# Four attention layers on one core: the values' weights loaded block by block, the first weights issued ahead, and PSUM banks dealt out anew

## The chip, the cores and the metric

The kernel runs on one core of a Trainium2 chip. The metric is the device time of one execution in microseconds, the median of several runs. The engines are TensorE (PE: matmuls, with PEld for its weight loads), VectorE (DVE), ScalarE (ACT), GpSimd (POOL) and SyncE (SP), whose queue issues every DMA of this kernel.

## The reference, cut to what matters

Four layers in the order A, B, A, B, each added to its input. Both normalise x (2048 tokens by 576 features), project to 32 heads of 18 features, and attend over all tokens; A has keys and values per head, B one key and one value head for all.

```python
def _A_ref(x, wqkv, wo):
    qkv = transpose((x @ wqkv).reshape(B, S, 3, H, Dh), 2, 0, 3, 1, 4)
    q, k, v = qkv[0], qkv[1], qkv[2]
    p = softmax(einsum("bhqd,bhkd->bhqk", q, k) * (Dh ** -0.5))
    o = einsum("bhqk,bhkd->bhqd", p, v)
    return transpose(o, 0, 2, 1, 3).reshape(B, S, D) @ wo

def _B_ref(x, wq, wk, wv, wo):          # k = x @ wk, v = x @ wv: one head
    ...

x = x + _A_ref(_layernorm(x), A_wqkv, A_wo)
x = x + _B_ref(_layernorm(x), B_wq, B_wk, B_wv, B_wo)
x = x + _A_ref(_layernorm(x), A_wqkv, A_wo)
x = x + _B_ref(_layernorm(x), B_wq, B_wk, B_wv, B_wo)
```

## The kernel before, in words

**Tiling.** The tokens lie in 16 chunks of 128 (`xo`), and the projections take them in four groups T of 512. Every operand of a projection is kept as two rounded parts, hi and lo (ten slots of 128 features: 0 to 4 hi, 5 to 9 lo), and a product of the two is 14 matmuls (`TERMS`, L31), the hi products first, those that need lo later. So each weight block that comes in by DMA (`raw`) is split by two instructions: a copy to hi (`copy`, L137 on ACT or L139 on POOL) and a subtraction to lo (L161). `load_w` (L142) does this for one block; with `spare` the split is put into the list `splits` and done when `finish_loads` (L172) is called, and without it right away.

**A chunk's way into a layer.** `stats` (L241) takes a chunk's mean and variance on DVE and the reciprocal root on POOL, `scaled` (L253) writes the normalised chunk on DVE (L256, L257), `trans` (L296) transposes it on PE in five matmuls: four into a bank of the tag e (L208) and the fifth into the bank `oacc` (L209). `split_rows` (L197) then makes hi on ACT (L200, L201) and lo on DVE (L202, L203). `advance` does one `trans` and then calls `ready`, which does statistics and scaling for two chunks ahead, and statistics for one more.

**Projections.** `project(T, t)` (L360) makes 128 rows of queries and keys for 512 tokens: 14 matmuls into a bank of the tag m (or e, for fillers), hi by ACT (L375), lo by DVE (L381; for fillers by ACT and POOL), and the store to memory on SP. In layer A the values come from `natural` (L212), 14 matmuls of 288 columns for half a chunk's features (L216), evicted by ACT (L420 or L423). In layer B the values come out of the projection t=4 and are transposed by `v_trans` (L408) into columns 128 to 255 of `oacc` (L410) and copied by DVE (L411).

**Attention.** In 704 phases per layer PE computes scores twice (L497 for the maxima that DVE takes, L506; L638 for the exponentials that ACT takes, L642) and multiplies by the values into `oacc` (L663). The order is written out by hand (`ORDERS`, `todo`, `weave`).

**Output.** `out_w(c)` (L278) projects a chunk of the attention's output in two halves by `natural`, each into an m tile of its own, and DVE adds each half to `xo` (L282). `out_t` (L268) prepares hi and lo of the next two chunks (L137 on ACT, L274 and L276 on DVE). The generator `outs` runs through the 16 chunks, and behind chunk 8 and chunks 9, 11, 13 and 15 it already does `ready` and `advance` for the next layer.

**Banks and buffers.** PSUM has eight banks: `oacc`, three of tag e, and two pairs of tag m (`mtile2`; `mtile` uses the first bank of a pair). SBUF tiles `ptile` are a ring of 15 (tag p), which holds raw weights, evicted projections (`ev`), exponentials and more.

**The opening.** Layer 0 loads x chunks 0 to 3, makes chunks 0 and 1 ready, and then loads `wqkv`'s three parts for queries and keys (five blocks each) by `load_a`, with copies on ACT and subtractions on POOL; between the parts it runs halves of the first two projections. At T=0 of both A layers all five blocks of the values' weights (`load_wsm`, two halves each) are loaded and split on POOL ahead of the first projection of the loop.

All engines run their instructions in the order of the program (`manual_schedule`).

Of the kernel before, what the change touches and what calls it, by code (L numbers as in the profile page):

```python
# [17 lines left out]
DH = D // H  # L18
# [50 lines left out]
def tile_kernel(ctx: ExitStack, tc: tile.TileContext, A_x, A_wqkv, A_wo, B_x, B_wq, B_wk, B_wv, B_wo, out):  # L69
# [62 lines left out]
    def ptile(name, shape=(P, 512), dt=F32):  # L132
        return pool.tile(list(shape), dt, tag="p", bufs=15, name=name)
# [7 lines left out]

    def load_w(c, dsts, srcs, n, hi, lo, spare):  # L142

        raw = pool.tile([P, 640], F32, tag="xh", bufs=2, name="raw") if spare else ptile("raw")
        if sum(s_.shape[1] for s_, _ in srcs) < n:
            nc.gpsimd.memset(raw[:, :n], 0.0)
        for s_, c0 in srcs:
            k = s_.shape[1]
            if c < 4:
                nc.sync.dma_start(raw[:, c0:c0 + k], s_[c * P:(c + 1) * P, :])  # L150
            else:
                nc.sync.dma_start(raw[:64, c0:c0 + k], s_[4 * P:, :])
                nc.sync.dma_start(raw[64:, c0:c0 + k], s_[4 * P:, :])

        def split():
            r = P if c < 4 else 64
            for dst, c0, k in dsts:
                w = dst.shape[1]
                rw = raw[:, c0:c0 + w * k].rearrange("p (w n) -> p w n", w=w)
                copy(hi, dst[:, :, c, :], rw)  # L160
                lo.tensor_tensor(dst[:r, :, 5 + c, :], rw[:r], dst.bitcast(F32)[:r, :, c, :], op=OP.subtract)  # L161
                if c == 4:
                    nc.gpsimd.memset(dst.bitcast(F32)[64:, :, 9, :], 0.0)

        if spare:
            splits.append(split)
        else:
            split()

    splits = []  # L170

    def finish_loads():  # L172
        while splits:
            splits.pop(0)()

    def load_wsm(c, src, hi=nc.gpsimd, lo=nc.gpsimd, spare=False):
        for h in range(2):
# [31 lines left out]
        nc.tensor.transpose(ps1[:, :P], last, ident)  # L209
        return ps4.rearrange("p (c t) -> p c t", t=P), ps1[:, :P]  # L210

    def natural(lhs, h, tile_f):  # L212

        ps = tile_f("psn")[:, :288]
        for i, (xc, wc) in enumerate(TERMS):
            nc.tensor.matmul(ps, lhs[:, xc, :], wsm[:, wc, h * 288:(h + 1) * 288],  # L216
                             start=i == 0, stop=i == len(TERMS) - 1)
            beat()
        return ps
# [21 lines left out]
    def stats(c):  # L241
        xc = xo[:, c, :]
        st = pool.tile([P, 2, nc.vector.BN_STATS_DIM], F32, name="st")
        for i in range(2):
            nc.vector.bn_stats(st[:, i, :], xc[:, i * 288:(i + 1) * 288])  # L245
        mv = pool.tile([P, 2], F32, bufs=4, name="mv")
        nc.vector.bn_aggr(mv, st)
        rs = pool.tile([P, 2], F32, bufs=4, name="rs")
        nc.gpsimd.tensor_scalar(rs[:, 0:1], mv[:, 1:2], EPS, None, op0=OP.add)
        nc.gpsimd.tensor_tensor(rs[:, 1:2], rs[:, 0:1], mhalf, op=OP.pow)  # L250
        return c, mv, rs
# [25 lines left out]

    def out_w(c):  # L278
        ot = ots_[c // 2][:, :, c % 2 * P:(c % 2 + 1) * P]
        for h in range(2):  # L280
            cs = slice(h * 288, (h + 1) * 288)
            nc.vector.tensor_tensor(xo[:, c, cs], natural(ot, h, mtile), xo[:, c, cs], op=OP.add)  # L282

    ors, ots_, lts, rls = {}, {}, {}, {}
    xhs = {}
# [10 lines left out]
    def trans(c):  # L296
        xh = xhs.pop(c)
        split_rows(xt_of(c), *transposed(xh, xh[:, 512:640]))


    at_chunk = {"stats": 0, "scaled": 0, "trans": 0}

    def ready(ahead=1):

        n = min(at_chunk["trans"] + 2, NCH)
        for what, m in (("stats", n), ("scaled", n), ("stats", min(n + ahead, NCH))):
            while at_chunk[what] < m:
                c = at_chunk[what]
                xhs[c] = stats(c) if what == "stats" else scaled(*xhs.pop(c))
                at_chunk[what] += 1  # L310

    def advance(n=1, ahead=1):
        for _ in range(n):
            trans(at_chunk["trans"])
            at_chunk["trans"] += 1
        ready(ahead)

    tail = []

# [28 lines left out]
    for layer in range(4):  # L348
# [56 lines left out]
        vts, half_done = [], {}  # L405

        def v_trans(T, vt):
            pv = oacc[:, P:2 * P]  # L408
            for u in range(4):
                nc.tensor.transpose(pv[:, u * 32:u * 32 + DH], vt[64:82, u * P:(u + 1) * P], ident[64:82, 64:82])  # L410
            nc.vector.tensor_copy(vs[0][:, 4 * T:4 * T + 4, 0, :DH],  # L411
                                  pv.rearrange("p (u e) -> p u e", u=4)[:, :, :DH])

        def v_dst(c, h):
            return v_of(c)[:, 16 * h:16 * h + 16, :DH]

        def project_v(c, h, tile_f, stage=None):
            pv = natural(xt_of(c), h, tile_f)
            if stage is None:
                nc.scalar.activation(v_dst(c, h), pv.rearrange("p (e d) -> p e d", d=DH), AF.Copy)  # L420
            else:
                stage.append((c, h, ptile("vst", (P, 288))))
                nc.scalar.activation(stage[-1][2], pv, AF.Copy)  # L423

# [95 lines left out]
        nc.gpsimd.memset(vs[0][:, :, :, DH:], 1.0)  # L522
        at_chunk.update(stats=0, scaled=0, trans=0)
        if layer == 0:
            ready(0)
            advance(2, 0)
            for c in range(5):
                load_a(c, (0,), nc.scalar, nc.gpsimd)
            load_x(2)
            for t in (0, 1):  # L530
                project(0, t, half=0)
            advance(2, 0)
            for c in range(5):
                load_a(c, (2,), nc.scalar, nc.gpsimd)
            load_x(3)
            for t in (0, 1):
                project(0, t, half=1)
            for c in range(5):
                load_a(c, (1,), nc.scalar, nc.gpsimd)
            load_x(4)  # L540
            ready()
        else:
            for c in outs:
                finish_loads()
                if is_a and 2 <= c < 7:
                    load_a(c - 2, (1,), spare=True)
                if c == 8:
                    ready()
                if c in (9, 11, 13, 15):
                    advance()  # L550

        def last_values():

            staged = []
            for c in range(8, 12):
                for h in range(2):
                    project_v(c, h, mtile, staged)
            vs.append(pool.tile([P, NV], F32, tag="vy", bufs=1, name="vy")
                      .rearrange("p (c h e) -> p c h e", c=NCH // 2, h=H))
            nc.gpsimd.memset(vs[1][:, :, :, DH:], 1.0)  # L560
            for c, h, t in staged:
                copy(nc.gpsimd, v_dst(c, h), t.rearrange("p (e d) -> p e d", d=DH))

        rest = [1, 2, 3, 5] if is_a else [2, 3]
        for T in range(4):
            if T == 0 and is_a:
                for c in range(5):
                    load_wsm(c, A_wqkv[:, 2 * D:])
                if layer == 0:
                    for tt in (5, 6, 7):  # L570
                        load_x(tt)
            elif T == 0:
                fixed_rows(k_slot(0), True)
                fixed_rows(q_slot(0), False)
            if is_a:
                ts = range(0 if T or layer else 2, 9) if T < 3 else (6, 7, 8, 0, 4)
            else:
                ts = (4, 0, 1, 2, 3) if T < 3 else (4, 0, 1)
            for i, t in enumerate(ts):
                if not is_a and T == 2 and i == 1:  # L580
                    woven(max_pair, 10, 5)
                elif not is_a and T == 3:
                    woven(max_pair, *((2, 7), (4, 3), (4, 3))[i])
                project(T, t, not is_a and T >= 2)
                if is_a and T == 3 and i == 2:
                    load_k(0, 0, 1536)
                    load_q(0, 0, 512)
                    last_values()

                if T < 3 and (i % 2 != (T + layer == 0) if is_a else i < 4):  # L590
                    advance()
                if not is_a and i < 2:
                    (load_q if i else load_k)(0, T * 512, T * 512 + 512)
                if vts and i != 0:
                    v_trans(*vts.pop())
            if is_a and T < 2:
                for c in range(4 * T, 4 * T + 4):
                    for h in range(2):
                        project_v(c, h, mtile)
        fill = []  # L600
        if is_a:
            for c in range(12, NCH):
                for h in range(2):
                    fill.append((project_v, (c, h, etile)))
        for t in rest:
            fill.append((project, (3, t, True)))

# [193 lines left out]
```

## Time and profile before

| | |
|---|---|
| median of three runs | 5880.99 us (5880.96 to 5881.37) |
| the profiled execution | 5882.09 us |
| its span, first to last instruction | 5880.3 us |
| PE busy | 5806.8 us, 99% of the span |
| DVE busy | 5181.1 us, 88% |
| ACT busy | 4608.6 us, 78% |
| POOL busy | 1731.2 us, 29% |
| mean granted clock of TensorE | 0.995 |
| first matmul of the values' projection in layer 0 | 72.2 us |

In the profile a line is "line engine operation out<-in shape xcount", with busy time or start and duration, and in brackets how long the engine stood idle before it and what released it. "PE psq L367 <- DVE ev L381" means that PE's matmul of L367 waited for DVE's instruction of L381. A view by stretches gives for each stretch its length, the busy time and number of instructions of PE, PEld, DVE, ACT and POOL, the granted clock (1.00 is full speed), the share of DMA time and GB/s.

### The profile page before, as it was taken

What the parts mean: (1) busy time and instruction counts of PE and PEld (TensorE: products, weight loads), DVE (VectorE), ACT (ScalarE), POOL (GpSimd) and SP (SyncE); (2) the same over time, 40 slices, a digit from 0 to 9 for tenths busy, and PEclk for the clock granted to TensorE, in tenths of its full rate; (3) what the DMA queues carried; (4) which work ended last, traced back from release to release, by engine and by line L of the source; (5) the groups of instructions that cost most, each with busy time, mean ns of one, the idle gap of its engine ahead of it and who ended that gap; (6) DMA issues with size and microseconds to landing.
All of it is one profiled execution on the core that took longest, in us unless ns stands there. A gap on an engine that the chain in (4) does not pass through costs nothing.

```text
span 5880.3 us, 132800 instructions
## 1 busy us (share of the span) xinstructions
PE 5806.8 (99%) x53756; PEld 2919.1 (50%) x53756; DVE 5181.1 (88%) x5385; ACT 4608.6 (78%) x8888; POOL 1731.2 (29%) x2222
## 2 busy tenths in 40 slices
PE   8999999999999999999999999999999999999999
PEld 7644444444744444444586444444447444444446
DVE  3699999998599999999647999999976999999995
ACT  2488888888278888888625888888882788888885
POOL 3133323233123323323311333232331333232332
PEclk9999999999999999999999999999999999999999
DMA  5311111111321000010243111111113200000002
GB/s 175 122 44 34 32 35 31 34 32 23 106 76 27 20 22 20 22 23 23 68 141 99 44 33 33 35 31 34 29 35 109 65 23 22 23 19 22 20 16 76
DMA packets 250307, 276.42 MB, mean 47 GB/s; under 512 B 131732, under 2 KB 171924, under 8 KB 239972
## 3 DMA queue, kind: packets, MB, share of 16 engines
q1 hardware_dynamic: 249692, 267.92, 16.3%
q8 instruction: 422, 6.91, 0.5%
q14 instruction: 193, 1.58, 0.1%
HBM read 151.24 MB, written 112.56 MB: 45 GB/s over the span
## 4 chain that ended last, share of the span: by engine, by line
PE 96%; DVE 2%; POOL 1%; DMA 1%; ACT 1%; issue 0%; SPq 0%; POOLq 0%; DVEq 0%; ACTq 0%
PE oacc L663 36%; PE psm L497 31%; PE pse L638 17%; PE psq L367 6%; PE psn L216 6%; DVE mx L506 0%; PE ps L208 0%; DVE st L245 0%; POOL big L161 0%; DMA raw<-in_A_wqkv_dram 0%; ACT pt L642 0%; DMA raw<-in_B_wk_dram 0%; DVE xh L256 0%; DVE yx L202 0%; POOL wsm L161 0%
## 5 line engine op out<-in xcount | busy, mean ns | idle before, releaser
L506 DVE TENSOR_REDUCE mx<-psm 128x2 f32<-128x1024 f32 x4096 | 4773.3, 1217 | 181.2 <-PE psm L497 143.7
L642 ACT ACTIVATE pt<-pse 128x512 f32<-128x512 f32 x8192 | 4315.4, 603 | 544.8 <-PE pse L638 372.8
L638 PE MATMUL pse<-big 64*128 64x512 f32 x8192 | 2451.9, 418 | 6.3 <-DMA big<-m_d 3.2
L497 PE MATMUL psm<-big 62*128 62x512 f32 x8192 | 2298.1, 453 | 5.6 <-DVE mx L506 5.4
L663 PE MATMUL oacc<-pt,vbuf 128*19 128x384 f32 (+1 forms) x24560 | 1754.8, 384 | 1.9 <-ACT oc L669 1.9
L497 PEld LDWEIGHTS psm<-big 62*128 62x128 f32 x8192 | 926.5, 184 | 1477.8 <-DVE mx L506 923.0
L638 PEld LDWEIGHTS pse<-big 64*128 64x128 f32 x8192 | 1188.3, 185 | 291.0 <-ACT pt L642 193.5
L663 PEld LDWEIGHTS oacc<-pt,vbuf 128*19 128x19 f32 x24560 | 500.5, 97 | 771.6 <-issue 593.9
L139 POOL TENSOR_SCALAR hl<-neg 128x8 fp32r<-128x8 f32 x256 | 50.6, 198 | 2679.0 <-DVE neg L614 2679.0
L663 PE MATMUL oacc<-pt,vy 128*19 128x256 f32 x8176 | 592.8, 384 | 0.0
L686 POOL TENSOR_TENSOR rl<-lt,mone 128x8 f32<-128x8 f32 x256 | 423.4, 1654 | 562.2 <-DMA lt<-os 562.1
L139 POOL TENSOR_SCALAR os<-oc 32x512 f32<-32x512 f32 x512 | 313.3, 612 | 130.0 <-ACT oc L669 87.9
L375 ACT ACTIVATE ev<-psq 128x512 fp32r<-128x512 f32 (+1 forms) x112 | 66.9, 598 | 354.1 <-PE psq L367 203.0
L699 POOL TENSOR_TENSOR os<-os,rb 96x512 f32<-96x512 f32 x256 | 328.5, 1283 | 21.4 <-DMA rb<-r_d 20.6
L677 POOL TENSOR_TENSOR os<-os,oc 96x512 f32<-96x512 f32 x256 | 327.1, 1278 | 21.3
L216 PE MATMUL psn<-wsm,xx 128*128 128x288 f32 x2240 | 320.3, 301 | 7.7 <-DVE xo L282 7.0
L216 PEld LDWEIGHTS psn<-wsm,xx 128*128 128x128 f32 x2240 | 305.1, 191 | 26.1 <-issue 13.9
L663 PEld LDWEIGHTS oacc<-pt,vy 128*19 128x19 f32 x8176 | 176.9, 98 | 250.7 <-issue 201.8
L381 DVE TENSOR_TENSOR ev<-psq,ev 128x512 fp32r<-128x512 f32 (+1 forms) x84 | 57.9, 692 | 230.5 <-ACT ev L375 204.0
L367 PE MATMUL psq<-yx,big 128*128 128x512 f32 (+2 forms) x812 | 215.0, 417 | 19.3 <-DVE ev L381 12.6
L367 PE MATMUL psq<-xx,big 128*128 128x512 f32 (+1 forms) x784 | 202.7, 404 | 0.0
L367 PEld LDWEIGHTS psq<-yx,big 128*128 128x128 f32 (+1 forms) x812 | 156.0, 203 | 60.2 <-DVE ev L381 13.5
(65 smaller groups left out, 1399.7 us busy)
## 6 DMA issues: line engine op xcount, KB each, us to landing
big<-qk_d SPq DMA_DIRECT2D x180, 432.0 KB
qk_d<-ev SPq DMA_DIRECT2D x96, 512.0 KB
qk_d<-ev SPq DMA_DIRECT2D x120, 256.0 KB
rb<-r_d SPq DMA_DIRECT2D x512, 36.0 KB
o_d<-os SPq DMA_DIRECT2D x512, 36.0 KB
m_d<-tr SPq DMA_DIRECT2D x1024, 2.0 KB
o<-o_d SPq DMA_DIRECT2D x64, 256.0 KB
big<-m_d SPq DMA_DIRECT2D x512, 4.0 KB
```

The source lines that it names most:

```text
L139: eng.tensor_scalar(dst, src, 1.0, 0.0, op0=OP.mult, op1=OP.add)
L216: nc.tensor.matmul(ps, lhs[:, xc, :], wsm[:, wc, h * 288:(h + 1) * 288], start=i == 0, stop=i == len(TERMS) - 1)
L367: nc.tensor.matmul(ps[:n].rearrange("p (u t) -> p u t", u=2)[:, us], w[:, wc, :n], xts[T][:, us, xc, :], start=j == 0, stop=j == len(TERMS ...
L375: nc.scalar.activation(ev[0][:n], ps[:n], AF.Copy)
L497: nc.tensor.matmul(ps[:, slot], q[b:b + KM, c0:c0 + P], k[b:b + KM, kb * 512:(kb + 1) * 512], start=True, stop=True)
L506: nc.vector.reduce_max(mxs[p, u][:, r0:r1 + 1:r1 - r0], ps, axis=AX.X)
L638: nc.tensor.matmul(e, k[r:r + KE, kc * P:(kc + 1) * P], q[r:r + KE, u * 512:(u + 1) * 512], start=True, stop=True)
L642: nc.scalar.activation(pt, e, AF.Exp, scale=SCALE)
L663: nc.tensor.matmul(oacc[j:j + DH + 1, cs], v_of(kc)[:, 2 * p + a if is_a else 0, :], pts[p, u, i][:, cs], start=kc < 2 and c0 == 0, stop=k ...
L677: nc.gpsimd.tensor_tensor(t[:96], t[:96], oc[:96], op=OP.add)
L686: nc.gpsimd.tensor_tensor(rl, lts.pop((p, u)), mone, op=OP.pow)
L699: nc.gpsimd.tensor_tensor(t[:96], t[:96], rb[:96], op=OP.mult)
```

## The change

- `load_w` always puts its split into `splits`; `finish_loads(n)` does the first n.
- The opening issues the DMAs of all 15 blocks of the first weights, with x chunks 4 to 9 between them, before anything else; copies stay on ACT, subtractions go to DVE, one part at a time between the projections' halves. Statistics and scaling of chunks 2 and 3 stand behind the split of the first part.
- At T=0 of the A layers one block of the values' weights is loaded behind each of the first five projections (in layer 0 also two x chunks behind each of the first three), and split behind the next one.
- `out_w` and the values' projection write both halves of a chunk into the two banks of one m pair, with one add (576 elements) or one eviction for both.
- `v_trans` writes into a bank of tag e in place of `oacc`.
- In `outs` the statistics of chunks 0 and 1 stand behind chunk 7, and the last `advance` behind chunk 14 in place of 15.

```diff
     def load_w(c, dsts, srcs, n, hi, lo, spare):
...
-        if spare:
-            splits.append(split)
-        else:
-            split()
+        splits.append(split)
...
-    def finish_loads():
-        while splits:
+    def finish_loads(n=99):
+        while splits and n:
             splits.pop(0)()
+            n -= 1
...
-    def natural(lhs, h, tile_f):
-
-        ps = tile_f("psn")[:, :288]
+    def natural(lhs, h, bank):
+
+        ps = bank[:, :288]
...
     def out_w(c):
         ot = ots_[c // 2][:, :, c % 2 * P:(c % 2 + 1) * P]
+        ps = mtile2("psn")
         for h in range(2):
-            cs = slice(h * 288, (h + 1) * 288)
-            nc.vector.tensor_tensor(xo[:, c, cs], natural(ot, h, mtile), xo[:, c, cs], op=OP.add)
+            natural(ot, h, ps[:, h])
+        xc = xo[:, c, :].rearrange("p (h n) -> p h n", h=2)
+        nc.vector.tensor_tensor(xc, ps[:, :, :288], xc, op=OP.add)
...
     def advance(n=1, ahead=1):
-        for _ in range(n):
-            trans(at_chunk["trans"])
-            at_chunk["trans"] += 1
-        ready(ahead)
+        more("trans", at_chunk["trans"] + n)
+        if ahead is not None:
+            ready(ahead)
...
         def v_trans(T, vt):
-            pv = oacc[:, P:2 * P]
+            pv = etile("psv")[:, :P]
...
+        def project_v(c):
+            ps = mtile2("psn")
+            for h in range(2):
+                natural(xt_of(c), h, ps[:, h])
+            return ps[:, :, :288].rearrange("p h (e d) -> p h e d", d=DH)
...
+        def project_v_part(c, h):
+            ps = natural(xt_of(c), h, etile("psn"))
+            nc.scalar.activation(v_dst(c)[:, h], ps.rearrange("p (e d) -> p e d", d=DH), AF.Copy)
...
         if layer == 0:
+            for part, tt in ((0, 2), (2, 3), (1, 4)):
+                for c in range(5):
+                    load_a(c, (part,), nc.scalar, nc.vector)
+                load_x(tt)
             ready(0)
-            advance(2, 0)
-            for c in range(5):
-                load_a(c, (0,), nc.scalar, nc.gpsimd)
-            load_x(2)
+            advance(2, None)
+            finish_loads(5)
+            ready(0)
             for t in (0, 1):
                 project(0, t, half=0)
-            advance(2, 0)
-            for c in range(5):
-                load_a(c, (2,), nc.scalar, nc.gpsimd)
-            load_x(3)
+            advance(2, None)
+            finish_loads(5)
             for t in (0, 1):
                 project(0, t, half=1)
-            for c in range(5):
-                load_a(c, (1,), nc.scalar, nc.gpsimd)
-            load_x(4)
+            finish_loads()
             ready()
...
-                if c == 8:
+                if c == 7:
+                    more("stats", 2)
+                elif c == 8:
                     ready()
-                if c in (9, 11, 13, 15):
+                elif c in (9, 11, 13, 14):
                     advance()
...
-            if T == 0 and is_a:
-                for c in range(5):
-                    load_wsm(c, A_wqkv[:, 2 * D:])
-                if layer == 0:
-                    for tt in (5, 6, 7):
-                        load_x(tt)
...
                 if T < 3 and (i % 2 != (T + layer == 0) if is_a else i < 4):
                     advance()
+                if T == 0 and is_a and i < 6:
+                    finish_loads()
+                    if i < 5:
+                        load_wsm(i, A_wqkv[:, 2 * D:])
+                    if layer == 0 and i < 3:
+                        load_x(5 + i)
...
             if is_a and T < 2:
                 for c in range(4 * T, 4 * T + 4):
-                    for h in range(2):
-                        project_v(c, h, mtile)
+                    nc.scalar.activation(v_dst(c), project_v(c), AF.Copy)
```

`more(what, m)` does statistics, scaling or transposes up to chunk m.

More of the change, by code (lines that the diff above doesn't have):

```diff
@@ L301, in tile_kernel, with more @@
     at_chunk = {"stats": 0, "scaled": 0, "trans": 0}
+    def more(what, m):
+        while at_chunk[what] < m:
+            c = at_chunk[what]
+            if what == "trans":
+                trans(c)
+            else:
+                xhs[c] = stats(c) if what == "stats" else scaled(*xhs.pop(c))
+            at_chunk[what] += 1
     def ready(ahead=1):
         n = min(at_chunk["trans"] + 2, NCH)
[L306 to L310, printed above, removed]
+        more("stats", n)
+        more("scaled", n)
+        more("stats", min(n + ahead, NCH))
     def advance(n=1, ahead=1):
-        for _ in range(n):
-            trans(at_chunk["trans"])
-            at_chunk["trans"] += 1
-        ready(ahead)
+        more("trans", at_chunk["trans"] + n)
+        if ahead is not None:
+            ready(ahead)
     tail = []
@@ L412, in v_trans, with v_dst @@
                                   pv.rearrange("p (u e) -> p u e", u=4)[:, :, :DH])
[L414 to L423, printed above, removed]
+        def project_v(c):
[3 more added lines that the diff above has]
+            return ps[:, :, :288].rearrange("p h (e d) -> p h e d", d=DH)
+        def v_dst(c):
+            return v_of(c)[:, :, :DH].rearrange("p (h e) d -> p h e d", h=2)
+        def project_v_part(c, h):
+            ps = natural(xt_of(c), h, etile("psn"))
+            nc.scalar.activation(v_dst(c)[:, h], ps.rearrange("p (e d) -> p e d", d=DH), AF.Copy)
         def q_slot(p):
@@ L555, in last_values @@
             for c in range(8, 12):
+                pv = project_v(c)
                 for h in range(2):
-                    project_v(c, h, mtile, staged)
+                    staged.append((c, h, ptile("vst", (P, 16, DH))))
+                    nc.scalar.activation(staged[-1][2], pv[:, h], AF.Copy)
             vs.append(pool.tile([P, NV], F32, tag="vy", bufs=1, name="vy")
@@ L561, in last_values @@
             for c, h, t in staged:
-                copy(nc.gpsimd, v_dst(c, h), t.rearrange("p (e d) -> p e d", d=DH))
+                copy(nc.gpsimd, v_dst(c)[:, h], t)
         rest = [1, 2, 3, 5] if is_a else [2, 3]
         for T in range(4):
-            if T == 0 and is_a:
-                for c in range(5):
-                    load_wsm(c, A_wqkv[:, 2 * D:])
-                if layer == 0:
-                    for tt in (5, 6, 7):
-                        load_x(tt)
-            elif T == 0:
+            if T == 0 and not is_a:
                 fixed_rows(k_slot(0), True)
@@ L603, in tile_kernel @@
                 for h in range(2):
-                    fill.append((project_v, (c, h, etile)))
+                    fill.append((project_v_part, (c, h)))
         for t in rest:
```

## The prediction

> **What bounds the kernel now.** I read the page first, its engine totals and slices, then what TensorE (PE) waits for, then busy time by stretches, and last the timeline around each wait.
>
> ```profile
> PE 5806.8 (99%) x53756; PEld 2919.1 (50%) x53756; DVE 5181.1 (88%) x5385; ACT 4608.6 (78%) x8888; POOL 1731.2 (29%) x2222
> ...
> PE   8999999999999999999999999999999999999999
> ...
> DVE  3699999998599999999647999999976999999995
> ```
>
> PE sets the time, so only PE's idle time and its slow clock can be won: 5880.3 - 5806.8 = 73.5 us idle, little of it in the attention loops, in which a stretch of 60 us reads 60.00 busy. What PE waits for:
>
> ```profile
> PE psq L367 <- DVE ev L381: 12.6, 3, 6.7
> PE oacc L410 <- DVE xx L203: 11.8, 4, 3.1
> PE ps L208 <- DVE xh L256: 9.8, 4, 6.3
> PE psn L216 <- DVE xo L282: 7.0, 9, 1.9
> PE oacc L410 <- DVE yx L203: 5.7, 2, 2.9
> ...
> PE psq L367 <- POOL big L161: 3.5, 4, 2.2
> ```
>
> Columns: us in all, times, longest. All these lie in three kinds of place: the opening, the passage from one layer to the next, and the projections of layers 1 and 3 (L410, 17.5 us). Busy time by stretches (PE, PEld, DVE, ACT, POOL, then the granted clock): the opening, the three passages, and two shorter stretches right behind a wait.
>
> ```profile
> 0.00:72.20 72.20, 46.60 (x194) 37.18 (x195) 32.58 (x71) 17.83 (x39) 40.34 (x76) 0.91 0.64 214
> 1518.54:1550.82 32.28, 28.20 (x188) 27.31 (x189) 20.32 (x51) 5.67 (x14) 4.55 (x11) 0.89 0.00 1
> 2930.73:2961.93 31.20, 26.99 (x190) 26.10 (x189) 20.38 (x51) 5.68 (x14) 4.70 (x11) 0.95 0.09 25
> 4443.49:4474.39 30.90, 26.79 (x190) 25.91 (x189) 20.34 (x51) 5.67 (x14) 4.56 (x11) 0.94 0.00 1
> 1562.55:1565.95 3.40, 3.40 (x9) 2.67 (x9) 0.87 (x4) 0.00 (x0) 0.79 (x2) 0.50 0.27 90
> 4484.40:4491.20 6.80, 6.12 (x17) 4.92 (x18) 2.57 (x8) 0.00 (x0) 0.79 (x2) 0.50 0.35 131
> ```
>
> The last two show that a wait is paid twice: for 3.4 or 6.8 us behind it the clock is 0.50, and PE is "busy" but half as fast. The timeline has the waits themselves:
>
> ```profile
> 13.29 5.01 POOL L161 TENSOR_TENSOR big<-raw,big 128x384 fp32r<-128x384 f32 x5
> 32.56 5.07 PE L367 MATMUL psq<-yx,big 128*128 128x512 f32 x14 [3.43 <-DVE ev L381]
> 63.15 8.75 PE L367 MATMUL psq<-yx,big 128*128 128x512 f32 x28 [6.75 <-DVE ev L381]
> 1519.68 0.66 PE L208 MATMUL ps<-ident,xh 128*128 128x128 f32 x4 [1.15 <-DVE xh L256]
> 1522.33 10.40 PE L216 MATMUL psn<-wsm,xx 128*128 128x288 f32 x56 [1.89 <-DVE xo L282]
> 1561.47 0.42 PE L410 MATMUL oacc<-ident,vt 18*128 18x18 f32 x4 [2.83 <-DVE xx L203]
> 1561.82 5.06 PE L367 MATMUL psq<-yx,big 128*128 128x512 f32 x14
> ```
>
> Fourteen matmuls of 512 columns take 3.5 us undisturbed (1570.97 to 1574.32) and 5.06 behind the wait: 1.6 us of clock.
>
> The profiled execution took 5882.09 us, span 5880.30 and 1.79 around it; the median of the runs is 5880.99, 1.10 lower. A measurement tells 0.2% (12 us) from no change.
>
> **Part 1, the opening (now 72.2 us to the first values' matmul).** The subtractions L161 (15 of 1.0 us) leave POOL, where they stood behind layernorm steps, for DVE. DVE's price for 128x384 from two SBUF inputs is not in the trace; L274 takes 0.684 us for 128x512, L276 0.422 for 64x256, so between them about 0.55 (an estimate). Upper bound 1.24, what DVE's L256 took while POOL split weights, instead of 0.58; below 0.42 nothing speaks for. I take 0.55, since POOL is nearly free there. The steps:
>
> - PE starts at 10.4 as now, paced by ACT's copies (0.43 apart) to 11.9. DVE's five run from 10.3 to 13.0, so the other 24 matmuls do not wait: at the cold 0.233 (19 in 4.42 us) they end at 17.5, now 23.25.
> - DVE: statistics of chunks 2 and 3 (2.0 us) and scaling (0.72 each), ready at 16.5. Their transposes with the wait for oacc take 2.6 as now: 20.1. Second halves 3.6: 23.7.
> - ACT copies part 2 (2.17 us) until 22.7, evicts t=0 by 23.3, t=1 by 24.4. DVE subtracts part 2 from 21.0 to 23.75, then evicts: 24.45 and 25.1. t=2 starts at 24.5 (0.8 idle; now 32.56) and ends at 28.0.
> - Queued behind on DVE: part 1 (2.75), statistics of chunks 4 and 5 (2.0), scaling. So transpose 4 starts at 30.4: a new wait of 2.4 us.
> - Transpose 0.9, then six projections of 3.5 and three transposes: 55.0. One half-rate window behind the new waits, 1.7: 56.7.
>
> SP issues part 1's six DMAs right behind the others, at 12.4 instead of 35.4; at the 286 to 362 GB/s that the DMA view shows for the first 12 us all 5.9 MB are in by 21, before ACT needs them (24). All 15 buffers of tag p hold weights at first; the first eviction takes one freed at 13.0. The values' blocks (POOL, 2 x 1.24 us each) no longer fill ten p buffers, nor stand as one block of 13 us in POOL's queue, which held ACT's evictions (49 to 56) and DVE's scaling until 60.6. On SP each block is moved behind the stores of its projection: the last, behind t=6's (about 46.5), is in by 50.5 and split by 54, just before its use at 55; POOL's memsets and x chunks 10 to 15 have slack, and in layer 2, with nine projections ahead of the values, all of this has: 0. Sum: 72.2 - 56.7 = -15.5; bounds: -19 (no half-rate window, warm earlier), -8 (splits of 1.24, hidden only in part 0).
>
> **Part 2, three passages.** Statistics 0 and 1 (2.0 us of DVE) move before chunk 8, so scaling 0 follows the subtractions of out_t at once: in the first passage adds end at 1515.6, out_t 1517.3, scaling 1517.9, and PE needs it at 1518.54. With a pair per chunk, chunk 10 waits for the add of chunk 8, long done, not for that of 9, which stood behind scaling and statistics. The last transpose goes before chunk 15, which covers the 0.62 that the first projection waited. One add of 576 for two of 288: 0.46 and 0.36 become about 0.76; at the kernel's end it can't hide behind the second half's matmuls: +0.3. Undisturbed, two chunks with a transpose take 8.24 us (1541.03 to 1549.49 less a 0.22 wait); three of these and one transpose more are 25.4. Now 32.28, 31.20 and 30.90: 94.4 - 76.2 = -18.2. I leave 0.7 for new small waits: -17.5. If scaling 0 is still late (idle 1.15 and half a window, 1.7, each): -9.6.
>
> **Part 3, L410's own bank.** It no longer waits for DVE to read oacc: -17.5, and the clock behind: 14 matmuls took 5.06, 5.09 and 6.05 for 3.5, two stretches at T=2 lose 1.7 and 2.9: -10.3. What is late next: at T=0 and 1 nothing, as per projection with its transposes DVE has 3.5 us (L381 0.69, L202 and L203 1.05, scaling 0.72, statistics 1.05) against PE's 4.4. At T=2 the three e banks also hold projections: the one behind psv reuses the bank that ACT is still emptying (two of 0.6 us, against 1.29 of PE work between): 0.3. And the maxima (1.23 each) make DVE nearly as full as PE: 1 us per layer. Sum -25; bounds -28, and -18 if both T=2 waits stay.
>
> The values' evictions (0.41 twice, now about 0.65 once) lie beside matmuls: 0.
>
> **Sum.** 5882.1 - 15.5 - 17.5 - 25 + 0.3 = 5824.4, less 1.1: 5823 us.
>
> **A rule against it.** The rows: 2.83 us idle were enough for a 3.4 us stretch at 0.50. The Trainium skill, "TensorE: Matmul & The Clock Gate", "HAM oscillation", warns of idle gaps longer than about 3.4 us; taken strictly, these waits would not slow the clock, and removing them would not bring it back. By the rows the trace speaks against that reading.
>
> **Rivals.**
>
> - The half-rate stretches are not due to the waits and stay: 10.3 in part 3, 18.2 - 12.5 idle = 5.7 in part 2, so 5823 + 16 = 5839. For it: a 2.88 us wait at 4509.7 had no such stretch. Against: eight stretches begin at such waits. 0.06. It is what that rule of the Trainium skill would make of this kernel.
> - Values' weights come late, since SP holds their issue behind stores that wait for DVE: the margin is 1 us, and 10 us late gives 5833: 0.05.
> - L410 still waits, for vt or by another order that keeps it behind L203: 25 back, 5848: 0.04.
> - Slower: the attention loops. DVE has 3% to spare there:
>
> ```profile
> 1740.00:1800.00 60.00, 60.00 (x602) 26.83 (x605) 58.31 (x58) 53.46 (x104) 31.77 (x47) 1.00 0.16 37
> ```
>
> The loop starts with other turns of the bank rings, and with DVE less far ahead. If PE then waited for L506 in each phase (704 a layer, 2816 in all), 21 ns a phase would eat 58 us; 30 ns make 84, 5907. Against: the order in the loop is unchanged, and L506 delays PE 5.4 us in the whole kernel. 0.04.
> - Gains and new waits cancel (DVE holds PE in the opening, each passage and T=2): 5881, 0.03.
>
> **Numbers.** Forecast 5823, chance 0.78, with its own bounds 5816 (-19, -18.2, -28) to 5846 (-8, -9.6, -18). The range 5814 to 5846 also holds the clock and late-weights cases. Faster by over 0.2%: 0.78 + 0.06 + 0.05 + 0.04 = 0.93; within: 0.03; slower: 0.04.
>
> **What would show it.** Right: no L410 among PE's waits, no L282 nor L256 at the passages, the first values' matmul near 57, passages of 26 us at a clock near 1.00, PE's idle time below 35. Part 1 wrong: L381 still ahead of t=4 or t=7, or values' matmuls waiting for POOL's wsm. The whole wrong: attention loops with PE waiting for L506.

## The result, and the profile after

The changed kernel takes 5818.78 us in the median of five runs (5815.04 to 5821.77), the kernel before 5880.99: a ratio of 0.9894 (0.9879 to 0.9908), 62 us less. The forecast was 5823 us, range 5814 to 5846. The profiled execution is the fastest of the five, 5815.04 us with a span of 5813.3, so its stages add up to 67 us less than before, not 62.

The page after, engine totals: PE has 5813.3 - 5783.1 = 30 us of idle time left of 73.5.

```profile
span 5813.3 us, 132695 instructions
...
PE 5783.1 (99%) x53756; PEld 2903.9 (50%) x53756; DVE 5173.7 (89%) x5336; ACT 4604.9 (79%) x8872; POOL 1714.7 (29%) x2207
```

What PE waits for after (in all, times, longest). L410, L282 and, but for 0.6 us, L381 are gone from the list; a late split of the values' weights (`wsm`) is new. Lines have moved: L207 is the transpose, L255 the scaling, L374 `project`, L215 `natural`, L388 the eviction's lo part, L417 `v_trans`, L506 and L515 the maxima on PE and DVE.

```profile
PE ps L207 <- DVE xh L255: 8.7, 2, 6.4
PE psm L506 <- DVE mx L515: 6.5, 8, 2.4
...
PE psn L215 <- POOL wsm L139: 1.6, 1, 1.6
...
PE psn L215 <- POOL wsm L164: 0.8, 1, 0.8
...
PE psq L374 <- ACT evr L385: 0.7, 2, 0.3
PE psq L374 <- DVE ev L388: 0.6, 1, 0.6
```

By stretches (length, then PE, PEld, DVE, ACT, POOL, granted clock, DMA): the opening, and the three passages from the first transpose to the next layer's first projection. PE no longer idles in a passage, and the clock is full.

```profile
0.00:51.52 51.52, 39.98 (x194) 32.92 (x195) 37.35 (x86) 17.71 (x39) 20.79 (x52) 0.97 0.85 273
1504.03:1528.48 24.45, 24.45 (x190) 24.45 (x189) 19.85 (x45) 5.75 (x14) 3.22 (x9) 1.00 0.00 1
2894.20:2918.65 24.45, 24.45 (x191) 24.45 (x189) 19.85 (x45) 5.75 (x14) 3.23 (x9) 1.00 0.00 1
4396.82:4421.27 24.45, 24.45 (x190) 24.45 (x189) 19.85 (x45) 5.75 (x14) 3.22 (x9) 1.00 0.00 1
```

The opening in the timeline: the splits on DVE, the new wait at transpose 4, and the two waits for the last block of the values' weights.

```profile
10.47 2.43 DVE L162 TENSOR_TENSOR big<-raw,big 128x384 fp32r<-128x384 f32 x5
...
10.49 5.66 PE L374 MATMUL psq<-yx,big 128*128 128x256 f32 x28 [0.78 <-ACT big L137]
...
28.44 1.12 PE L207 MATMUL ps<-ident,xh 128*128 128x128 f32 x4 [2.29 <-DVE xh L255]
...
51.52 1.40 PE L215 MATMUL psn<-wsm,yx 128*128 128x288 f32 x8
...
54.54 0.40 PE L215 MATMUL psn<-wsm,yx 128*128 128x288 f32 x1 [1.62 <-POOL wsm L139]
...
55.79 6.38 PE L215 MATMUL psn<-wsm,yx 128*128 128x288 f32 x36 [0.84 <-POOL wsm L164]
```

From the start times in the timelines the whole can be cut into stages, PE's time in us. "Passage" is from the end of a layer's attention to the next layer's first projection, "projections" from there to the first multiplication by the values. In layer 0 the first projection starts at 10.4 us before and at 10.5 after.

| | before | after | difference |
|---|---|---|---|
| layer 0, projections with the opening | 234.5 | 218.1 | -16.4 |
| passages to layers 1, 2, 3 | 62.2, 62.0, 60.8 | 54.2, 54.2, 54.2 | -22.4 |
| layers 1 and 3, projections | 109.8, 110.5 | 97.1, 97.1 | -26.1 |
| layer 2, projections | 204.3 | 204.1 | -0.3 |
| attention, four layers | 4969.9 | 4967.9 | -2.0 |

### The profile page after: what moved, and what is told of

Its sections match the earlier page's. It is cut to its first block, busy times and chain, and to the rows that moved or that the text cites. A ratio compares the mean times of both kernels' runs of the same rounds, so it can differ in the third digit from the quotient of the medians.

```text
span 5813.3 us, 132695 instructions
## 1 busy us (share of the span) xinstructions
PE 5783.1 (99%) x53756; PEld 2903.9 (50%) x53756; DVE 5173.7 (89%) x5336; ACT 4604.9 (79%) x8872; POOL 1714.7 (29%) x2207
## 4 chain that ended last, share of the span: by engine, by line
PE 97%; DVE 1%; DMA 0%; POOL 0%; ACT 0%; issue 0%; SPq 0%; POOLq 0%; ACTq 0%; DVEq 0%
PE oacc L674 36%; PE psm L506 31%; PE pse L649 17%; PE psn L215 6%; PE psq L374 6%; DVE mx L515 1%; PE ps L207 0%; DMA raw<-in_B_wk_dram 0%; ACT pt L653 0%; PE oacc L208 0%; SPq L151 0%; POOL big L162 0%; DMA raw<-in_A_wqkv_dram 0%; DVE xh L255 0%; DVE st L244 0%
## 5 line engine op out<-in xcount | busy, mean ns | idle before, releaser
L515 DVE TENSOR_REDUCE mx<-psm 128x2 f32<-128x1024 f32 x4096 | 4771.9, 1217 | 172.8 <-PE psm L506 130.6
L506 PE MATMUL psm<-big 62*128 62x512 f32 x8192 | 2296.7, 453 | 6.8 <-DVE mx L515 6.5
L506 PEld LDWEIGHTS psm<-big 62*128 62x128 f32 x8192 | 926.5, 184 | 1480.1 <-DVE mx L515 926.9
L215 PE MATMUL psn<-wsm,xx 128*128 128x288 f32 x2240 | 313.3, 297 | 0.0
L215 PEld LDWEIGHTS psn<-wsm,xx 128*128 128x128 f32 x2240 | 299.3, 188 | 15.9 <-issue 15.6
L388 DVE TENSOR_TENSOR ev<-psq,ev 128x512 fp32r<-128x512 f32 (+1 forms) x84 | 58.0, 690 | 217.4 <-ACT ev L382 201.7
L374 PE MATMUL psq<-yx,big 128*128 128x512 f32 (+2 forms) x812 | 200.2, 397 | 2.1 <-ACT big L137 0.8
L374 PE MATMUL psq<-xx,big 128*128 128x512 f32 (+1 forms) x784 | 201.0, 401 | 0.0
L680 ACT ACTIVATE oc<-oacc 128x512 f32<-128x512 f32 x256 | 158.2, 618 | 28.2 <-PE oacc L674 28.2
```

Of the source, the lines that this page charges most:

```text
L374: nc.tensor.matmul(ps[:n].rearrange("p (u t) -> p u t", u=2)[:, us], w[:, wc, :n], xts[T][:, us, xc, :], start=j == 0, stop=j == len(TERMS ...
L506: nc.tensor.matmul(ps[:, slot], q[b:b + KM, c0:c0 + P], k[b:b + KM, kb * 512:(kb + 1) * 512], start=True, stop=True)
L515: nc.vector.reduce_max(mxs[p, u][:, r0:r1 + 1:r1 - r0], ps, axis=AX.X)
L680: nc.scalar.activation(oc, oacc, AF.Copy)
```

## The experiments

All are edits of the changed kernel. Medians and ratios to the kernel before are of runs that alternate with it; stage times are from one profile each. Where their code is unchanged, the passages (54.2 us) and the projections of layers 1 and 3 (97.1 to 97.4) come out alike, so that 2 us are plain there. The projections of layer 0 do not: with the code of the changed kernel they take 218.1, 218.7, 218.9, 220.5 and 220.7 us in five profiles, as the half-rate stretches and the wait for wsm fall.

### Small transposes back in oacc

```diff
-            pv = etile("psv")[:, :P]
+            pv = oacc[:, P:2 * P]
```

> The changed kernel with one part undone: v_trans writes into oacc again. Theory (a wait is paid twice, as idle time and as half-rate clock behind it): the six waits of 2.8 to 3.1 us for L202 come back with half-rate stretches of 3.4 or 6.8 us behind most of them, the stretch from the first projection to the first multiplication by the values grows from 97.1 us to 109 to 111 in layers 1 and 3, and the whole by 24 to 28 us. Rival 1 (the clock does not hang on waits this short): only the idle time comes back, 106 us in each of the two layers, the whole by 17 to 18 us, and no half-rate stretch there. Rival 2 (DVE would hold PE there anyway): under 5 us.

Measured: 5844.22 us, ratio 0.9937 (0.9922 to 0.9951). The projections of layers 1 and 3 take 110.5 and 111.1 us. PE's waits, and a stretch right behind the first of them:

```profile
PE oacc L417 <- DVE xx L202: 11.7, 4, 3.1
...
PE oacc L417 <- DVE yx L202: 5.7, 2, 2.9
```

```profile
1540.30:1547.10 6.80, 6.39 (x18) 5.11 (x19) 2.30 (x8) 0.00 (x0) 0.79 (x2) 0.50 0.32 119
```

The two stages grow by 27.4 us, of which 17.4 are shown as waiting; five of the six waits have a stretch of 3.4 or 6.8 us at clock 0.50 that begins within 0.7 us of their end. So the waits are paid twice, and the rival with a clock that doesn't hang on such waits (106 us per layer) falls.

### First weights split on POOL

```diff
-                    load_a(c, (part,), nc.scalar, nc.vector)
+                    load_a(c, (part,), nc.scalar, nc.gpsimd)
```

> The changed kernel with the first weights' subtractions on POOL, everything else as changed (all DMAs still issued ahead). Theory (the engine of the splits matters): five subtractions take 5.0 us in place of 2.4 and stand ahead of the layernorm's POOL steps of chunks 2 and 3; the first values' matmul comes at 56 to 60 us in place of 51.5, the whole 4 to 8 us longer. Rival (issuing the DMAs ahead is what counts): the first values' matmul within 1.5 us of 51.5.

Measured: 5824.49 us, 0.9904 (0.9889 to 0.9919); values' first matmul at 59.5 us, projections of layer 0 8.8 us longer than the changed kernel's (226.9), and 6 longer than the slowest of the five profiles. By the medians it is 5.7 us, with intervals that overlap, so the stage is the firmer reading. In the timeline POOL's five subtractions take twice as long, and transpose 4 waits 6.0 us, as DVE's scaling waits for layernorm steps queued behind the splits on POOL:

```profile
10.49 4.83 POOL L162 TENSOR_TENSOR big<-raw,big 128x384 fp32r<-128x384 f32 x5 [3.75 <-ACT big L137]
35.77 1.12 PE L207 MATMUL ps<-ident,xh 128*128 128x128 f32 x4 [5.99 <-DVE xh L255]
```

Of the 20.7 us by which the values start earlier (72.2 to 51.5), 8.0 are the engine's; what remains (72.2 to 59.5) comes with the weights issued ahead, the order and the values' blocks, which this run does not separate.

### A chunk's halves apart; and the old order

Two kernels, each with one of the two edits of the passage undone.

```diff
-        ps = mtile2("psn")
         for h in range(2):
-            natural(ot, h, ps[:, h])
-        xc = xo[:, c, :].rearrange("p (h n) -> p h n", h=2)
-        nc.vector.tensor_tensor(xc, ps[:, :, :288], xc, op=OP.add)
+            cs = slice(h * 288, (h + 1) * 288)
+            nc.vector.tensor_tensor(xo[:, c, cs], natural(ot, h, mtile("psn")), xo[:, c, cs], op=OP.add)
```

> The changed kernel with out_w as before: each half in a tile of its own and an add for each; the new order of statistics stays. Theory (both the pair and the order were needed): chunk 10's first half waits for the add of chunk 9, which stands behind scaling 0 and 1 and statistics 2: about 0.9 us, and 0.2 to 0.5 at each later chunk behind a transpose; the passages take 55.5 to 58 us in place of 54.2, the whole 4 to 11 us more. Rival (the order alone is enough): passages within 0.5 us of 54.2.

```diff
-                if c == 7:
-                    more("stats", 2)
-                elif c == 8:
+                if c == 8:
                     ready()
-                elif c in (9, 11, 13, 14):
+                elif c in (9, 11, 13, 15):
                     advance()
```

> The changed kernel with the order of the next layer's first steps as before (statistics 0 and 1 behind chunk 8, the last advance behind chunk 15); the pairs stay. Theory: transpose 0 waits 1.1 us for scaling again and the first projection 0.6, without the 1.9 us behind it; passages of 56 to 58 us in place of 54.2, the whole 5 to 11 us more, depending on whether a half-rate stretch follows. Rival (the pair alone is enough): passages within 0.5 us of 54.2.

Measured: with the halves apart 5825.45 us, 0.9904 (0.9888 to 0.9921), passages of 56.2, 56.7 and 56.2; with the old order 5824.74, 0.9903 (0.9888 to 0.9918), passages of 56.6, 56.7 and 56.6. PE's waits in the passage to layer 1, first halves apart, then old order:

```profile
PE psn L215 <- DVE xo L281: 1.1, 2, 0.9
PE psq L372 <- DVE xo L281: 0.3, 1, 0.3
```

```profile
PE ps L207 <- DVE xh L255: 1.4, 1, 1.4
PE psq L374 <- issue: 0.6, 1, 0.6
```

Either edit alone leaves 2.0 to 2.5 us of the loss per passage, so both were needed. Undone singly they cost 2.0 + 2.4 us in the first passage; undone together, in the kernel before, 8.0. Most of the difference of 3.6 is the clock: in these passages no half-rate stretch follows one wait of 0.9 or 1.4 us, while one of 6.8 us followed 1.15 and 1.89 in a row, and the 56 matmuls behind them took 10.40 us against 7.67 in the changed kernel, 2.7 more.

### Values' weights in one block

```diff
+            if T == 0 and is_a:
+                for c in range(5):
+                    load_wsm(c, A_wqkv[:, 2 * D:])
+                    finish_loads()
...
-                if T == 0 and is_a and i < 6:
-                    finish_loads()
...
```

> The changed kernel with the values' weights loaded and split in one block ahead of the projections of the A layers, as before; the rest of the opening as changed. Theory (one block per part was needed): POOL works 13 us on end and ten of the 15 p buffers wait for it, so evictions and scaling stand still as before; the first values' matmul of layer 0 comes 4 to 9 us later than 51.5, the whole 2 to 6 us more, since the wait of 2.5 us for late values' weights and its half-rate stretch go. Rival (with the first weights in early the block does no harm): the values start by 52, without the 2.5 us wait, and the whole is 2 to 4 us less.

Measured: 5818.22 us, 0.9888 (0.9873 to 0.9902), no difference from the changed kernel that can be told, where 2 to 6 us more were expected. The values start at 57.9 in place of 51.5, with one long wait ahead of them:

```profile
49.45 8.19 PE L374 MATMUL psq<-yx,big 128*128 128x512 f32 x28 [4.31 <-DVE ev L388]
```

In exchange PE doesn't wait for wsm. The projections of layer 0 take 220.6 us, within the 218.1 to 220.7 of the changed code. So the block does hold evictions up, as the theory had it, but splitting one block per part wins nothing that can be told where it was put: its own wait of 2.5 us, and the clock behind it, takes the gain.

### Values' weights one projection earlier

```diff
+                if T == 0 and is_a and i < 6:
+                    finish_loads()
+                    if i < 5:
+                        load_wsm(i, A_wqkv[:, 2 * D:])
+                    if layer == 0 and i < 3:
+                        load_x(5 + i)
                 project(T, t, not is_a and T >= 2)
...
-                if T == 0 and is_a and i < 6:
...
```

> The changed kernel with each block of the values' weights issued and split one projection earlier (ahead of the projection, so ahead of its stores on SP). Theory (the late weights, 2.5 us of waiting and a half-rate stretch at 55, come from SP's order): the waits for wsm go, the projection stage of layer 0 takes 213 to 215 us in place of 218.1. Rival (POOL's splits are what is late): at most 1 us less.

Measured: 5812.29 us, 0.9876 (0.9861 to 0.9891), projections of layer 0 212.9 us, 5.2 less than in the changed kernel's profile. With this edit the stage takes 212.8 to 215.2 us in three profiles, without it 218.1 to 220.7 in five, so that the gain is clear and its size is not. The wait shrinks to one of 0.37:

```profile
50.07 1.45 PE L215 MATMUL psn<-wsm,yx 128*128 128x288 f32 x9
51.89 13.34 PE L215 MATMUL psn<-wsm,yx 128*128 128x288 f32 x98 [0.37 <-POOL wsm L164]
```

The rival, by which POOL's splits are what is late, allowed 1 us at most. In the changed kernel each block was issued on SP behind the stores of its projection: the first at 31.6 us (24.1 with this edit), since SP stood 3.9 us at the store of t=2's lo part, for DVE's L388; the last from 49.3 (44.8 with this edit), behind t=6's stores, which begin at 48.2. POOL's copies of the last two blocks waited for these loads:

```profile
51.14 0.43 POOL L139 TENSOR_SCALAR wsm<-raw 128x288 fp32r<-128x288 f32 x1 [1.27 <-DMA raw<-in_A_wqkv_dram]
...
54.06 0.43 POOL L139 TENSOR_SCALAR wsm<-raw 128x288 fp32r<-128x288 f32 x1 [0.32 <-DMA raw<-in_A_wqkv_dram]
```

That speaks for SP's order. But the edit moves POOL's splits forward as well, and in the changed kernel POOL also stood 3.7 us (to 41.3) at a layernorm step ahead of the second block's split; how the gain divides between the two queues is not shown. The intervals of the two ratios overlap (0.9879 to 0.9908 for the changed kernel), so the stage is the firmer reading.

### Layernorm of chunks 4 and 5 ahead of the third part

```diff
-            finish_loads()
             ready()
+            finish_loads()
```

> The changed kernel with the statistics and scaling of chunks 4 and 5 ahead of the split of the third part in the opening. Theory (the new wait of 2.3 us at transpose 4 comes from DVE's queue and is paid twice): the wait and the half-rate stretch at 28 go, the values' first matmul comes at 47.5 to 49 in place of 51.5; but the values' weights then come later against it, so their wait grows to 3 to 6 us; the whole 0 to 4 us less. Rival (the wait moves on to the eviction or the split of part three): values' first matmul within 1 us of 51.5.

Measured: 5821.12 us, 0.9894 (0.9878 to 0.9911): nothing. The wait at transpose 4 is gone, the values start at 50.0, and the time comes back at once:

```profile
32.08 3.53 PE L374 MATMUL psq<-yx,big 128*128 128x512 f32 x14 [1.12 <-DVE ev L388]
...
53.00 1.44 PE L215 MATMUL psn<-wsm,yx 128*128 128x288 f32 x5 [2.34 <-POOL wsm L139]
55.69 0.61 PE L215 MATMUL psn<-wsm,yx 128*128 128x288 f32 x1 [1.25 <-POOL wsm L139]
56.93 8.36 PE L215 MATMUL psn<-wsm,yx 128*128 128x288 f32 x48 [0.63 <-POOL wsm L164]
```

Theory and rival were each right in part: half of the wait moves to an eviction (1.1), and the values' weights are later against it (4.2 in place of 2.5). The start at 50.0 lies between the two forecasts of it.

### Next layer's weights split a step later

Before and after, attention of layers 0 and 2 takes 1244 to 1247 us, that of layers 1 and 3 1239. The timeline of the changed kernel shows why, in part: POOL stands at a split that waits for a load of `wk`; the negated maxima (`hl`) are behind it, DVE's transpose of them waits, then the maxima, then PE.

```profile
1336.57 0.40 POOL L139 TENSOR_SCALAR big<-raw 128x256 fp32r<-128x256 f32 x1 [2.96 <-DMA raw<-in_B_wk_dram]
...
1337.75 0.20 POOL L139 TENSOR_SCALAR hl<-neg 128x8 fp32r<-128x8 f32 x1
1338.03 0.20 POOL L629 TENSOR_TENSOR hl<-neg,hl 128x8 fp32r<-128x8 f32 x1
1338.27 0.21 DVE L634 STREAM_TRANSPOSE tr<-hl 128x32 f32<-128x32 f32 x1 [2.46 <-POOL hl L629]
...
1339.64 0.80 PE L506 MATMUL psm<-big 62*128 62x512 f32 x2 [2.40 <-DVE mx L515]
```

```diff
-                at(b - 29, finish_loads)
-                at(b + 3, finish_loads)
+                at(b - 28, finish_loads)
+                at(b + 4, finish_loads)
```

> The changed kernel with the splits of the next layer's weights one step (some 1.7 us) later in the attention loop. In the changed kernel and in the one before, PE stands still 2.3 us near 1340 (1357 before) with a half-rate stretch behind: POOL waits for a small slow load of wk, the negated maxima stand behind that wait, then DVE, then PE. Theory: that wait goes, and with it 2.4 us of idle time and 1.7 to 5 us of clock per A layer: attention stages of layers 0 and 2 near 1240 in place of 1244 to 1246, the whole 5 to 12 us less, and the runs lie closer together than 5815 to 5822. Rival (another load or queue holds POOL): stages stay at 1244 or more.

Measured: 5811.93 us, 0.9877 (0.9862 to 0.9892); attention of layers 0 and 2 at 1242.9 and 1242.6. PE's longest wait for the maxima falls from 2.4 to 0.5:

```profile
PE psm L506 <- DVE mx L515: 2.2, 6, 0.5
```

The mechanism holds, its size was too large: 2.8 us in layer 0 (1245.7 to 1242.9) and 1.8 in layer 2 (1244.4 to 1242.6), where 4 to 6 in each were expected. Over the changed kernel's profile and those of its edits the two stages take 1241 to 1243 us with the later splits and 1243 to 1248 without, so this size is rough; other waits (2.8 us for rows of `m_d`) are there in its place. The median is 6.9 us below the changed kernel's (10 by the ratios), more than these account for, and the intervals of the ratios overlap (0.9862 to 0.9892 against 0.9879 to 0.9908), so the size by the medians stays open. Their spread says nothing on it: the kernel before itself lies in 1.2 us in one session and in 8.7 in another.

### Together

> The changed kernel with the values' weights one projection earlier and the splits of the next layer's weights one step later. If both gains (some 6.5 us each by the medians) come from different waits they add up: 5804 to 5808 us, PE without waits for wsm beyond 0.5 us and for the maxima beyond 2.5 us. If they share one cause or the half-rate stretches fall elsewhere: 5809 to 5812.

> The same with statistics and scaling of chunks 4 and 5 ahead of the third part's split. Theory (earlier values' weights leave room for it): 1 to 3 us less than without it. Rival (as when it was tried alone, the wait moves on to an eviction and to the values' weights): no difference beyond 1.5 us.

Measured: the two edits together (earlier values' weights, later splits) 5805.97 us, 0.9870 (0.9855 to 0.9884), and the waits for wsm are gone. By the medians the gains add up (6.5 and 6.9 us alone, 12.8 together); by the ratios they do so only in part (0.0018 and 0.0017 alone, 0.0024 together). The kernel before ran 3 us slower beside the single edits than beside this one, and the intervals hold both readings, so adding up is likely, not shown. With the layernorm of chunks 4 and 5 ahead as well 5802.59, 0.9863 (0.9846 to 0.9879), the fastest kernel here, 16 us below the changed one; its wait for wsm is 0.6 us. The third edit is worth nothing alone and 3.4 us by these medians once the weights come earlier. The runs of the two kernels lie apart, but the two intervals overlap, and the projections of layer 0 take 212.8 us against 212.9 with the earlier weights alone, so that last step is likely, not shown.

## Why the prediction was right

**The opening: right sum, by errors that cancel.** Expected -15.5, measured -16.4 for the stage. The DVE split was to cost 0.55 us and costs 0.552, the five end at 12.9 (13.0), the new wait at transpose 4 is 2.29 (2.4), and the half-rate stretch behind it cost about 1.45 (28 matmuls in 7.70 us for 6.75, and 0.5 in the transposes) of the 1.7 set down. Yet the values started at 51.5, 5.2 us before the forecast. Of that 2.0 came ahead of transpose 4 (28.4 for 30.4): PE was taken as cold through all first halves, ending at 17.5, but the full clock came at 14.4 (the matmuls start 0.21 us apart up to there and 0.12 behind it) and they ended at 16.15. About 3.0 came behind it: six projections and three transposes were summed by their listed durations, 3.5 and 0.9, which include the tail of a group that the next one overlaps; two projections with a transpose take 7.05 us from start to start (37.42 to 44.47), not 7.9. Of the 5.2 gained, 4.3 were given back: the values' last block was to be split by 54 and was by 57.5, and the waits of 1.62 and 0.84 came with a half-rate stretch. That is the rival of late weights, small and inside the forecast's case; the step that failed is the margin of 1 us. Values' matmuls that wait for wsm were also one of the prediction's own signs that this part is wrong, and by that sign it was: that the sum came out is luck.

**The passages: mechanism right, size too small, beyond the bound.** Expected -17.5 with -18.2 as the most; measured -22.4. The mis-sized term is the undisturbed time of a passage: 25.4 us by the prediction, 24.45 in fact, three times 0.95. It came from two chunks of 8.46 us less a wait shown as 0.22; without a wait they take 7.97 (1504.49 to 1512.46), so that wait cost 0.49. The idle time before a matmul counts from the modelled end of the one before, about 0.4 us long, while matmuls follow each other at 0.13; the weight loads' row, which said 0.46 for the same wait, was the one to use. The rest, 1.3 us, lies ahead of the first transpose: 0.8 behind a wait shown as 0.52 in the second passage, for which the prediction had nothing, and 0.17 in each passage, since their stretches were counted from the modelled end of the matmul before. The margins held: scaling 0 ended at 1503.5 and was needed at 1504.0; the whole-chunk add takes 0.755 us (0.76).

**L410: right.** Expected -25 with bounds -18 to -28, measured -26.1; what is late next was named with its size: 0.3 us at the e bank (two waits of 0.7 us in all), and 0.5 for the maxima in each of layers 1 and 3, where 1 was allowed. The run with oacc confirms both halves of the term, idle time and clock.

**The end of the kernel.** +0.3 expected: from PE's last matmul to the end of the span 3.74 us, before 3.44.

**The clock rule.** The Trainium skill's rule ("TensorE: Matmul & The Clock Gate", "HAM oscillation") was read strictly as one way to 5839. The runs differ from that reading: gaps of 2.8 to 3.1 us at the small transposes were followed by half rate in five of six cases, in the kernel before and again in the run with oacc.

**The rivals.** L410 does not wait for anything else. The attention loops did not slow down: 4967.9 us against 4969.9. The late weights came true in the small.

**Against the median.** The stages of the profiled execution give -67, the medians -62.2. The forecast of -57.7 was short by 4.9 us in the passages, and by 1 each in the opening and for L410; 2.3 more came from the attention loops and layer 2, for which it had nothing. The forecast is 4 us from the median, but 9 from the profile by whose stages it is checked here, the fastest of five.

## What to carry to other kernels

Where one engine sets the time, go by its waits and not by shares: PE was 99% busy, and of the 67 us won 43 were its idle time and 24 its busy time, most of that half-rate clock (stretches of 61 us in all before, 24 after). Here each wait of some 3 us cost about half as much again in clock. Two small waits next to each other can cost more than their sum, so remove both before judging either. When work is moved to be issued later, look at the queue that issues it: a block behind a store waits for that store's producers, here 3.9 us for an eviction on DVE.

## What the runs showed of the hardware that was not expected

The same wait does not always bring the half-rate clock. The 2.3 us at transpose 4 did so in the changed kernel (28.1 to 31.5), but not with the values' weights earlier, where the wait is 2.30 as well; the 2.4 us near 1340 were followed by 10.2 us at half rate in the changed kernel's profile, the 2.3 near 1356 by 3.4 in that of before. A wait need not be long either: one of 1.4 us at 4249.8 in the run with the halves apart was followed by 3.4 us at half rate. Just ahead of layer 0's first multiplication by the values every profile has waits of 0.33, 0.17 and 0.40 us within 3 us; in four of the twelve a stretch of 3.4 or 6.8 us at half rate begins there, in the others none. What decides whether such a stretch comes, and how long it is, no run here settles.
